# A two-layer network on attention output: the first sixteen feature steps issued from one written list of small pieces

## The chip, the core and the metric

The kernel runs on one core of a Trainium2 chip. The time is device time in microseconds (us) of one execution, taken as the median of the runs shown. A profile of one further execution gives the trace that is read here. Engines are named as in the profile: PE (matrix products), DVE (VectorE), ACT (ScalarE), POOL (GpSimd) and SP, whose queue issues nearly all DMAs.

## What is computed

Attention between 8 batches of 512 tokens and 32 state vectors per head, in both directions, then two feed-forward layers over all 8 x (512 + 32) = 4352 rows.

```
scores  = x @ state^T / 8;  a  = softmax(scores)      xread = a  @ state
scores2 = state @ x^T / 8;  a2 = softmax(scores2)     sread = a2 @ x
y = concat(xread, sread) as rows of 512
y = relu(y @ w_in)^2 @ w_out                          (512 -> 2048 -> 512, weights in float64)
h = y @ w2_in;  z = h * softmax(h)                    (512 -> 1024)
out = (z - mean) / sqrt(var + 1e-6) * g_ln @ w2_out   (1024 -> 512)
```

Every product keeps float32 accuracy by splitting each operand into a high and a low part and adding three products (high x high, high x low, low x high): lines 140, 141 and 142 of the kernel before.

## The kernel before, in words

**Layer 1, the feature steps.** The first layer is not applied to xread but to the attention weights: state @ w_in ("sw") is formed once per batch, so that the hidden values of a batch are a @ sw. There are 16 feature steps of 128 features for each batch. A step (b, f) has two parts. `hidden` makes six products of 128x512 into a bank `ps_h` (2 banks), ACT takes relu, then squares twice (`high`: `gh` and `r`), DVE subtracts (`low`: `gl`), and `project` multiplies `gh`, `gl` with four column blocks of w_out into four banks `acc` (twelve products). The steps of the first two batches alternate in chunks of four features: (0, 0 to 3), (1, 0 to 3), (1, 4 to 7), (0, 4 to 7) and so on. These first 16 steps are what the change is about. Each step's projection runs two steps behind its hidden product, so the work of the first 16 steps ends on PE with the fourteenth projection, just ahead of the seventeenth hidden product.

**Conversions.** w_in and w_out come as float64 words. A tile of 128x512 of them (0.5 MB) is converted by `convert_parts` in three parts: DVE does two masks and a multiply-add, ACT rebiases the exponent (`cz`); DVE joins the sign (`ch`), ACT writes the high part; DVE does a mask and a multiply for the low part. That is six DVE and two ACT instructions. 25 such conversions (13 of w_in, 12 of w_out) belong to the first 16 steps. Each converted w_in tile is also written to DRAM (`w1i_d`), and multiplied with the state (`sw_part`, products `ps_sw`, copied by ACT to `ev_sw` and stored to `sw_d`). `load_sw` reads a chunk of `sw_d` back into `stg`, and `split_sw` splits it (ACT high part, DVE low part) for the hidden products.

**Attention of a batch.** Transposes of x (`ps_x`), splitting (`xh`, `xl`, through a product with the negated identity, `negi`), scores (`ps_s`, copied to `st`), transposes by token (`ps_r`), row softmax (`rows_a`, `rows_b`, tiles `mx`, `e`, `sm`), transposes of the weights (`ps_a1`, shown as `ps_a`; split into `ah`, `al`), column softmax (`cols_a`, `cols_b`, tiles `cm`, `cs`), transposes of that (`ps_c`) and sread (`ps_sr`).

**Order.** The program is written as calls in a loop, and a scheduler of the framework decides the order on each engine, by its own estimates and by which buffers are free. Each engine then runs its instructions strictly in that order and waits where an operand is late. Layer 2 (line 743 on) comes after all 16 steps of 8 batches.

Of the kernel before, what the change touches and what calls it, by code (L numbers as in the profile page):

```python
# [8 lines left out]
F32 = mybir.dt.float32  # L9
# [11 lines left out]
def memory_attention_relu2_solu(  # L21
# [179 lines left out]
    def convert_parts(st, hi_r, lo_r, done=None):  # L201

        hi, lo = st[:, :, 1], st[:, :, 0]
        z = cvp.tile([P, 512], F32, tag="ce", name="cz")
        zu, zi = z.bitcast(U32), z.bitcast(I32)


        nc.vector.tensor_scalar(out=zu, in0=hi, scalar1=0x7FFFFE00, scalar2=None, op0=ALU.bitwise_and)
        nc.scalar.activation(out=zi, in_=zi, func=AF.Relu, scale=8.0, bias=rebias)

        u = cvp.tile([P, 512], F32, tag="cw", name="cu", bufs=4)
        uu = u.bitcast(U32)
# [90 lines left out]
    def sw_part(u, j):  # L303
# [106 lines left out]
        loading[b, c] = st  # L410

    def split_sw(b, c):
        st = loading.pop((b, c))
        loaded[b, c] = []
        for q in range(NQ):
            t = sw_tile("sw")
            split(t[:, 0, :], t[:, 1, :], st[:, q, :])
            loaded[b, c].append(t)

    def load_w1in(c, kk):  # L420
        for k in (2 * kk, 2 * kk + 1):
# [14 lines left out]
    def attention(b):  # L436

        v = {}

        def trans_x(hp):  # L440
            ps = bank("ps_x")
            transposes(ps, [xs_t[b][:, t, 2 * hp : 2 * hp + 2].rearrange("p h d -> p (h d)") for t in range(NT)])
            xh = xtp.tile([P, S], F32R, tag="xh", name="xh")
            xl = xtp.tile([P, S], F32R, tag="xl", name="xl")
            (split_bank if b < 2 else split)(xh, xl, ps)
            v["xt"] = (xh, xl)

        def scores_t(hp):
            xh, xl = v.pop("xt")
            q, i = hp // 2, hp % 2  # L450
            if i == 0:
                v["st", q] = atp.tile([P, S], F32, tag="st", name="st")
            if b < 2:
                if i == 0:
                    v["ps", q] = bank("ps_s")
# [90 lines left out]
                )  # L546

        def trans_a(q):
            if q == 0:
                a1_t[b] = (  # L550
                    a1p.tile([P, NQ, S], F32R, tag="ah", name="ah"),
                    a1p.tile([P, NQ, S], F32R, tag="al", name="al"),
                )
# [3 lines left out]
            (split_bank if b < 2 else split)(a1_t[b][0][:, q, :], a1_t[b][1][:, q, :], ps)  # L557

        def at(f, *a):
            return lambda: f(*a)  # L560
# [104 lines left out]
    fetch_pair(0, 0)  # L665
    load_x(0)
# [7 lines left out]
    fetch_pair(0, 1)  # L674
    fetch_pair(2, 0)
    fetch_pair(2, 1)
    fetch_w1out(0)
    att = attention(0)
    state_step(a_st, 0)
    load_x(1)  # L680
    for u in range(NM):
        begin("i", u)
        for k in range(5):
            advance()
            if k % 2 == 0 and len(att) > 5:
# [12 lines left out]
    begin("o", 0)
    load_state_rows(a_st, 2, B, nc.sync)
    state_step(a_st, 1)  # L700
    for u in range(NM):
        sw_part(u, 1)
        advance()
    while att:
        for piece in att.pop(0):
            piece()
    while flying:
        advance()
    nc.sync.dma_start(out=gcol, in_=g_ln.rearrange("(k p) -> p k", p=P))


# [103 lines left out]
    items += [(b, f) for b in range(2, B + 1) for f in range(NF)]  # L815
    chunks = [(b, c) for b, f in items if f % FPC == 0 for c in [f // FPC]]

    when = {("o", f): w for f, w in zip(range(1, NF), (0, 1, 2, 5, 6, 7, 8, 11, 12, 13, 14, 17, 19, 21, 22))}
    when |= {("i", u): w for u, w in zip(range(AHEAD, NU), (0, 1, 2, 3, 7, 8, 9, 10, 13, 15, 16, 18))}
    units = {}  # L820
    for unit, w in when.items():
        units.setdefault(w, []).append(unit)
# [10 lines left out]
            w2.append(t)  # L833

    done = []
    for s, (b, f) in enumerate(items):
        w, ws = divmod(s, NF)
        for kind, u in [unit for w_ in ((0, 1, 2) if s == 0 else (s + 2,)) for unit in units.get(w_, [])]:
# [37 lines left out]
        if s == 0:  # L876
            att = attention(1)
        if s in (11, 12):
            state_step(a_st, s - 9)
        if s == 2 * FPC - 2:  # L880
            load_sw(*chunks[2])
        for _ in range(4 if s < FPC else 1):
            if att:
                for piece in att.pop(0):
                    piece()
        if ws == 0 and 1 <= w < B - 1:
            load_x(w + 1)
        n = S if b < B else NSR
# [3 lines left out]
        done.append((b, f))  # L892
        if s // FPC + 1 < len(chunks) and chunks[s // FPC + 1][0] < B:
            nxt = chunks[s // FPC + 1]
            if s // FPC == 1:
                pass
            elif s % FPC == 1:
                if nxt not in loading:
                    load_sw(*nxt)
            elif s % FPC == 2:  # L900
                split_sw(*nxt)
        for e in ends.get(b, ())[1:]:
            i = f - e + 3
            if i not in (0, 1):
# [13 lines left out]
        for m in range(4):  # L918
# [5 lines left out]
                late_part(late, m - 2)  # L924
            if job:
                project(*job, m)
        if s == 2 * FPC - 1:
            split_sw(*chunks[2])
        if f == 0 and b == B - 1:
            sa.close()  # L930
            pools["x"] = pool("xp", 2, side="right")
# [69 lines left out]
```

## Time and profile before

| | |
|---|---|
| time, median of 3 runs (range) | 1135.21 us (1134.79 to 1138.87) |
| the profiled execution: its own time | 1133.88 us |
| its span in the trace | 1131.8 us |
| PE busy | 1102.5 us, 97% of the span |
| DVE busy | 704.0 us, 62% |
| ACT busy | 513.4 us, 45% |
| granted PE clock, mean of the span | 0.995 of full speed |

The span runs from the first to the last recorded event; the execution's own time has 2.1 us around it. Busy time of PE counts the modelled durations of its products, which overlap: a 128x512 product lasts 0.39 us, and the next one starts 0.23 us after it. So a busy PE may still be slow, when its clock is at the lower of its two levels (1.2 and 2.4 GHz; 0.5 and 1.0 in the profile).

### The profile page before, as it was taken

Reading aid. Unit: us, or ns where it says so; the run is one execution under the profiler, and the core shown is the slowest. Engines: PE = TensorE matmul, PEld = TensorE weight load, DVE = VectorE, ACT = ScalarE, POOL = GpSimd, SP = SyncE. Lnnn points to the kernel's source line nnn. Section 1 sums busy time; section 2 is a strip of 40 time slices with the busy share of each in tenths; the row PEclk is TensorE's granted clock in tenths of the full one; section 3 lists DMA queues with packets and bytes.
Section 4 is the critical chain, followed back from the end, with each engine's and each line's share of the span. In section 5 each row is a group of like instructions: output and inputs, shape, how many; then the busy total and the mean of one; then the engine's idle time right before and its main releaser. Section 6 shows DMA issues by size and latency. Waiting matters only on the chain.

```text
span 1131.8 us, 15153 instructions
## 1 busy us (share of the span) xinstructions
PE 1102.5 (97%) x5692; PEld 910.0 (80%) x5692; DVE 704.0 (62%) x1357; ACT 513.4 (45%) x903; POOL 44.7 (4%) x62
## 2 busy tenths in 40 slices
PE   5889999999999999999999999999999999999998
PEld 3667888888888888888888889988888888888886
DVE  6788886579477587784775446664545545445442
ACT  5878886456355353442343113443433434334332
POOL 1000000001000000010000000000000000000000
PEclk9899999999999999999999999999999999999999
DMA  9658874577666742422211127420101101000000
GB/s 291 236 177 280 298 238 135 168 225 216 208 208 174 210 146 75 140 75 60 72 38 57 38 75 256 153 75 19 61 24 57 66 19 45 21 19 28 19 28 28
DMA packets 92873, 134.69 MB, mean 119 GB/s; under 512 B 44800, under 2 KB 45312, under 8 KB 92800
## 3 DMA queue, kind: packets, MB, share of 16 engines
q1 hardware_dynamic: 92224, 133.59, 36.8%
q8 instruction: 45, 0.74, 0.3%
q14 instruction: 28, 0.23, 0.1%
q10 hardware_dynamic: 576, 0.13, 0.1%
HBM read 83.37 MB, written 49.28 MB: 117 GB/s over the span
## 4 chain that ended last, share of the span: by engine, by line
PE 91%; DVE 3%; ACT 3%; DMA 2%; issue 1%; SPq 0%; POOLq 0%; POOL 0%; ACTq 0%; DVEq 0%
PE h L750 16%; PE acc L140 11%; PE acc L141 10%; PE acc L142 10%; PE ps_h L140 6%; PE ps_h L141 6%; PE ps_h L142 6%; PE ps_o L801 5%; PE ps_o L799 5%; PE ps_o L800 5%; PE ps_t L789 2%; PE ps_sr L534 1%; PE ps_x L131 1%; DMA st<-in_moe_w_in_dram 1%; DMA st<-in_moe_w_out_dram 1%; PE ps_a L131 1%
## 5 line engine op out<-in xcount | busy, mean ns | idle before, releaser
L140 PE MATMUL acc<-gh,w1out 128*128 128x512 f32 (+1 forms) x576 | 218.8, 380 | 1.4 <-ACT ev_x L634 1.4
L141 PE MATMUL acc<-gl,w1out 128*128 128x512 f32 (+1 forms) x576 | 218.1, 379 | 0.0
L142 PE MATMUL acc<-gh,w1out 128*128 128x512 f32 (+1 forms) x576 | 217.8, 378 | 0.0
L750 PE MATMUL h<-w,x2h 128*128 128x512 f32 x544 | 148.6, 395 | 0.0
L593 ACT ACTIVATE r<-ps_h 128x512 f32<-128x512 f32 (+1 forms) x144 | 82.4, 573 | 141.2 <-PE ps_h L142 139.5
L595 DVE TENSOR_TENSOR r<-r,ps_h 128x512 f32<-128x512 f32 (+1 forms) x112 | 72.5, 647 | 88.9 <-ACT r L593 88.3
L140 PEld LDWEIGHTS acc<-gh,w1out 128*128 128x128 f32 x576 | 108.4, 188 | 22.3 <-ACT ev_x L634 1.8
L142 PEld LDWEIGHTS acc<-gh,w1out 128*128 128x128 f32 x576 | 108.4, 188 | 20.6
L141 PEld LDWEIGHTS acc<-gl,w1out 128*128 128x128 f32 x576 | 108.4, 188 | 20.0
L750 PEld LDWEIGHTS h<-w,x2h 128*128 128x128 f32 x544 | 99.6, 188 | 18.9
L609 DVE TENSOR_TENSOR gl<-r,gh 128x512 fp32r<-128x512 f32 (+1 forms) x144 | 96.5, 670 | 20.9 <-ACT r L602 17.9
L140 PE MATMUL ps_h<-ah,sw 128*128 128x512 f32 x256 | 107.8, 422 | 0.5 <-ACT r L593 0.5
L799 PE MATMUL ps_o<-w,lh 128*128 128x512 f32 x272 | 106.1, 390 | 1.0 <-ACT lh L119 1.0
L801 PE MATMUL ps_o<-w,ll 128*128 128x512 f32 x272 | 106.2, 390 | 0.6 <-DVE ll L120 0.6
L800 PE MATMUL ps_o<-w,lh 128*128 128x512 f32 x272 | 105.8, 389 | 0.0
L768 ACT ACTIVATE e<-h,nm 128x1024 f32<-128x1024 f32 x34 | 38.0, 1117 | 143.7 <-DVE nm L765 143.7
L141 PE MATMUL ps_h<-al,sw 128*128 128x512 f32 x256 | 101.3, 396 | 0.0
L142 PE MATMUL ps_h<-ah,sw 128*128 128x512 f32 x256 | 100.8, 395 | 0.0
L764 DVE TENSOR_REDUCE nm<-h 128x1 f32<-128x1024 f32 x34 | 41.6, 1225 | 84.4 <-PE h L750 84.4
L750 PE MATMUL h<-w,x2l 128*128 128x512 f32 x272 | 83.7, 389 | 0.0
L776 ACT ACTIVATE j<-e,mu 128x1024 f32<-128x1024 f32 x34 | 39.1, 1151 | 54.3 <-DVE mu L773 50.4
L801 PEld LDWEIGHTS ps_o<-w,ll 128*128 128x128 f32 x272 | 51.0, 188 | 12.0 <-DVE ll L120 1.5
(161 smaller groups left out, 1724.8 us busy)
## 6 DMA issues: line engine op xcount, KB each, us to landing
stg<-sw_d SPq DMA_DIRECT2D x120, 128.0 KB, 3.4
sw_d<-ev_sw SPq DMA_DIRECT2D x28, 512.0 KB, 3.7
st<-in_moe_w_out_dram SPq DMA_DIRECT2D x24, 512.0 KB, 5.2
xs<-in_x_dram SPq DMA_DIRECT2D x32, 256.0 KB, 4.0
w1i_d<-w1in SPq DMA_DIRECT2D x16, 512.0 KB, 4.5
st<-in_moe_w_in_dram SPq DMA_DIRECT2D x16, 512.0 KB, 5.8
w1in<-w1i_d SPq DMA_DIRECT2D x32, 256.0 KB, 4.7
x_d<-ev_x SPq DMA_DIRECT2D x16, 512.0 KB, 2.8
```

What stands on the lines that cost most here:

```text
L140: nc.tensor.matmul(out=ps, lhsT=lh, rhs=rh, start=first and i == 0, stop=False)
L141: nc.tensor.matmul(out=ps, lhsT=lh, rhs=rl, start=False, stop=False)
L142: nc.tensor.matmul(out=ps, lhsT=ll, rhs=rh, start=False, stop=last and i == n - 1)
L593: nc.scalar.activation(out=r, in_=ps, func=AF.Relu)
L595: nc.vector.tensor_tensor(out=r, in0=r, in1=ps, op=ALU.mult)
L609: nc.vector.tensor_tensor(out=gl, in0=r, in1=gh.bitcast(F32), op=ALU.subtract)
L750: nc.tensor.matmul(out=ps[:, a * 512 : (a + 1) * 512], lhsT=lt[:, k, t * P : (t + 1) * P], rhs=w2[k][:, i, a * 512 : (a + 1) * 512], start ...
L764: nc.vector.tensor_reduce(out=nm, in_=ps, axis=AX.X, op=ALU.max)
L776: nc.scalar.activation(out=j, in_=e, func=AF.Square, bias=mu, accum_out=var)
L799: nc.tensor.matmul(out=ps, lhsT=a, rhs=wt[:, 0, o : o + 512], start=(k == 0), stop=False)
L800: nc.tensor.matmul(out=ps, lhsT=a, rhs=wt[:, 1, o : o + 512], start=False, stop=False)
L801: nc.tensor.matmul(out=ps, lhsT=bb, rhs=wt[:, 0, o : o + 512], start=False, stop=(k == NK - 1))
```

## The change

Everything up to the end of the sixteenth feature step is no longer called in the loop, but from a written list of 304 entries. Each entry is one small piece, of a few instructions: a letter for the kind and hexadecimal digits for batch, step, unit or block. `T00` transposes the x of batch 0, pair of heads 0; `N00` is the second half of its split; `S` scores, `R` and `Q` the two halves of the row softmax, `A` and `B` the weights' transpose and the second half of its split, `C`, `D`, `E`, `F` the column direction; `i0` or `o0`, three times each, are the three parts of a conversion; `W10` is `sw_part` of unit 1 for j = 0; `V00` half a `split_sw`; `H`, `G`, `L` and `P` are `hidden`, `high`, `low` and one column block of `project`; `I`, `J`, `K`, `O`, `X`, `Z`, `l` are loads; `U` is a `state_step`. While the list is traced, PE, DVE, ACT and SP keep the list's order; later work is ordered by the scheduler as before, and may be put between entries of the list.

Banks and buffers change with it: the transposed x of the first two batches goes to the four `acc` banks (before: the two banks `m`), `sw_part` of the first four units to the `ps_h` banks (before: `acc` banks), `xh` and `xl` of batch 0 to buffers of `gh` and `gl`, those of batch 1 to that batch's `ah` and `al`, and `st` has four buffers (before: two). One conversion of w_in (unit 13) moves from the sixteenth step to the seventeenth. The load of `g_ln` now stands ahead of all other loads.

```diff
     def split_bank(hi, lo, ps):
 
         nc.scalar.activation(out=hi, in_=ps, func=AF.Copy)
-        nc.tensor.matmul(out=ps, lhsT=negi, rhs=hi, start=False, stop=True, skip_group_check=True)
-        nc.scalar.activation(out=lo, in_=ps, func=AF.Copy)
+
+        def rest():
+            nc.tensor.matmul(out=ps, lhsT=negi, rhs=hi, start=False, stop=True, skip_group_check=True)
+            nc.scalar.activation(out=lo, in_=ps, func=AF.Copy)
+
+        return rest
...
-        ps = ps_a.tile([P, 512], F32, tag=f"acc{hp}", name="ps_sw") if u < AHEAD and j < 2 else bank("ps_sw")
+        ps = ps_h.tile([P, 512], F32, tag="h", name="ps_sw") if u < AHEAD else bank("ps_sw")
...
         def trans_x(hp):
-            ps = bank("ps_x")
+            ps = ps_a.tile([P, 512], F32, tag=f"acc{hp}", name="ps_x") if b < 2 else bank("ps_x")
...
-    when = {("o", f): w for f, w in zip(range(1, NF), (0, 1, 2, 5, 6, 7, 8, 11, 12, 13, 14, 17, 19, 21, 22))}
-    when |= {("i", u): w for u, w in zip(range(AHEAD, NU), (0, 1, 2, 3, 7, 8, 9, 10, 13, 15, 16, 18))}
+    when = {("o", f): w for f, w in zip(range(12, NF), (20, 21, 22, 23))}
+    when |= {("i", u): w for u, w in zip(range(3 * AHEAD + 1, NU), (16, 17, 18))}
...
+    def piece(p):
+        k, a = p[0], [int(c, 16) for c in p[1:]]
+        if k in "TNSRQABCDEF":
+            att[a[0]][k](a[1])
...
+    PLAN = """
+    I0 X0 J0 I2 i0 J2 X1 i0 U0 O0 O1 T02 T00 i0 i1 N02 T03 i2 N00 Z W00 S02 T01 N03 i2 N01 i1 i1 S00 i3 S03
+    W10 i2 S01 T10 i3 i3 o0 W20 T11 N10 R00 o0 o1 W30 N11 I6 R01 o1 S10 T12 S11 Q00 Q01 I4 U1 o1 V00 V10 N12
+    A00 T13 o0 A01 B00 V00 V10 J4 B01 W01 N13 H00 O2 O3 i6 W11 G00 S12 H01 S13 i4 W21 i6 i6 L00 i5 W31 R10
...
+    with tc.manual_schedule(engines={getattr(mybir.EngineType, e) for e in ("PE", "DVE", "Activation", "SP")}):
+        for p in PLAN.split():
+            piece(p)
```

Three places show how the order on an engine moves. The first is PE ahead of the first hidden product (`ps_h`), before. `ps_a` is the transpose of the row softmax `e`, once for each half.

```order
L131 MATMUL ps_a_345<-ident,e_297 128x128 x2
L131 MATMUL ps_a_345<-ident,e_329 128x128 x2
L131 MATMUL ps_a_372<-ident,e_297 128x128 x2
L131 MATMUL ps_a_372<-ident,e_329 128x128 x2
L125 MATMUL ps_a_345<-ah,negi 128x512
L140 MATMUL ps_h<-ah,sw 128x512
L125 MATMUL ps_a_372<-ah,negi 128x512
L141 MATMUL ps_h<-al,sw 128x512
```

The same place of PE in the changed kernel, where lines have moved by 4 or more (L140 is L144, L131 is L135, L125 is L127).

```order
L135 MATMUL ps_a_464<-ident,e_380 128x128 x2
L135 MATMUL ps_a_464<-ident,e_410 128x128 x2
L135 MATMUL ps_x<-ident,xs 128x128 x4
L135 MATMUL ps_a_478<-ident,e_380 128x128 x2
L135 MATMUL ps_a_478<-ident,e_410 128x128 x2
L127 MATMUL ps_a_464<-ah,negi 128x512
L127 MATMUL ps_a_478<-ah,negi 128x512
L144 MATMUL ps_sw<-w1in,bd_1_155 128x512
L145 MATMUL ps_sw<-w1in,bd_1_155 128x512
L146 MATMUL ps_sw<-w1in,bd_1_155 128x512
L127 MATMUL ps_x<-ah,negi 128x512
L144 MATMUL ps_h<-ah,sw 128x512
```

The x of batch 1 (`ps_x`) and the first `sw_part` of the second state block (`bd_1`) now stand ahead of the first hidden product; before, all of batch 1's attention came after it. Ahead of these rows stand three more groups of batch 1's transposes, two of its score triples and the second `state_step`.

The second place is DVE at the same point, before: the end of the row softmax (`sm`, `e`), the low parts of the four `sw` tiles, the rest of a conversion, and three `low`.

```order
L498 TENSOR_SCALAR sm<-sm 128x16
L499 RECIPROCAL sm<-sm 128x16 x2
L500 TENSOR_TENSOR e_297<-e_297,sm 128x512
L500 TENSOR_TENSOR e_329<-e_329,sm 128x512
L516 RECIPROCAL cs<-cs 128x1
L120 TENSOR_TENSOR sw<-stg,sw 128x512 x4
L225 SCALAR_TENSOR_TENSOR w1out<-cu,cz 128x512
L609 TENSOR_TENSOR gl<-r,gh 128x512 x3
```

The same point of DVE in the changed kernel.

```order
L517 TENSOR_SCALAR sm<-sm 128x16
L518 RECIPROCAL sm<-sm 128x16
L519 TENSOR_TENSOR e_410<-e_410,sm 128x512
L120 TENSOR_TENSOR bd_1_155<-ps_st,bd_1_155 128x2x128
L120 TENSOR_TENSOR bd_1_158<-ps_st,bd_1_158 128x2x128
L228 TENSOR_SCALAR cz<-ch 128x512
L229 SCALAR_TENSOR_TENSOR w1out<-cu,cz 128x512
L120 TENSOR_TENSOR sw<-stg,sw 128x512 x2
L228 TENSOR_SCALAR cz<-ch 128x512
L229 SCALAR_TENSOR_TENSOR w1out<-cu,cz 128x512
L120 TENSOR_TENSOR sw<-stg,sw 128x512 x2
```

The column direction (`cs`, `cm`) has left this place for a later one, and the second `state_step` (`bd_1`) and two conversions of w_out finish ahead of the last `sw` split.

The third place is the start of SP's queue, before.

```order
L656 DMA st64w<-in_moe_w_in_dram 128x1024
L434 DMA xs<-in_x_dram 128x8x64 x4
L656 DMA st64w<-in_moe_w_in_dram 128x1024 x3
L163 DMA st_190<-in_moe_w_out_dram 128x1024
L434 DMA xs<-in_x_dram 128x8x64 x4
```

The start of SP's queue in the changed kernel.

```order
L697 DMA gcol<-in_moe_g_ln_dram 128x8x1
L681 DMA st64w<-in_moe_w_in_dram 128x1024
L441 DMA xs<-in_x_dram 128x8x64 x4
L681 DMA st64w<-in_moe_w_in_dram 128x1024 x3
L441 DMA xs<-in_x_dram 128x8x64 x4
L167 DMA st_217<-in_moe_w_out_dram 128x1024
L167 DMA st_219<-in_moe_w_out_dram 128x1024
```

`gcol` has come to the front, and the x of batch 1 has moved ahead of the first w_out tile.

## Rows read from the trace of the kernel before

**Rows 1.** The page: span, and busy time of each engine.

```profile
span 1131.8 us, 15153 instructions
PE 1102.5 (97%) x5692; PEld 910.0 (80%) x5692; DVE 704.0 (62%) x1357; ACT 513.4 (45%) x903; POOL 44.7 (4%) x62
```

**Rows 2.** Busy time by stretches; clock is a share of full, DMA of 16 engines.

```profile
core 0: us, PE busy (x) PEld busy (x) DVE busy (x) ACT busy (x) POOL busy (x), PEclk, DMA share, GB/s
0.00:7.21 7.21, 0.00 (x1) 0.04 (x1) 3.02 (x7) 2.72 (x4) 4.07 (x12) 1.00 0.84 203
7.21:26.13 18.92, 15.56 (x56) 9.76 (x56) 13.98 (x30) 12.75 (x26) 0.00 (x0) 1.00 1.06 334
26.13:30.90 4.77, 0.00 (x2) 0.03 (x1) 4.77 (x16) 3.81 (x8) 0.00 (x0) 0.83 0.98 308
68.86:72.18 3.32, 0.00 (x1) 0.03 (x1) 3.32 (x12) 1.62 (x3) 0.00 (x0) 1.00 0.00 0
138.57:200.00 61.43, 61.37 (x287) 50.43 (x286) 45.66 (x89) 44.47 (x80) 0.00 (x0) 1.00 0.60 189
200.00:1131.80 931.80, 925.75 (x4805) 772.17 (x4804) 546.79 (x1034) 361.14 (x623) 40.65 (x50) 1.00 0.30 94
```

**Rows 3.** The same view, from the first hidden product to the seventeenth.

```profile
33.44:138.57 105.13, 97.29 (x538) 75.65 (x537) 88.68 (x183) 86.81 (x163) 0.00 (x0) 0.97 0.71 238
```

**Rows 4.** The same view, PE alone, where its clock was low.

```profile
33.44:36.40 2.96, 2.96 (x9) 0.55 0.84 153
29.60:36.40 6.80, 5.50 (x17) 0.52 0.95 283
74.00:77.40 3.40, 3.26 (x9) 0.55 0.43 166
```

**Rows 5.** PE's waits, 0 to 260 us: for whom, total, times, longest.

```profile
PE ps_a L131 <- DVE e L500: 8.1, 2, 4.8
```

**Rows 6.** PE in order of time: start, duration, instruction.

```profile
33.44 0.63 PE L140 MATMUL ps_h<-ah,sw 128*128 128x512 f32 x1
...
112.85 0.60 PE L289 MATMUL ps_st<-ident,a_st 128*128 128x128 f32 x4
113.21 0.48 PE L140 MATMUL ps_h<-ah,sw 128*128 128x512 f32 x1
...
138.35 0.39 PE L142 MATMUL acc<-gh,w1out 128*128 128x512 f32 x1
138.57 0.39 PE L140 MATMUL ps_h<-ah,sw 128*128 128x512 f32 x1
```

**Rows 7.** DVE in order of time, with the idle time before and its cause.

```profile
10.98 0.43 DVE L208 TENSOR_SCALAR cz<-st64w 128x512 uint32<-128x512 uint32 x1 [1.73 <-DMA st64w<-in_moe_w_in_dram]
...
16.00 0.42 DVE L208 TENSOR_SCALAR cz<-st64w 128x512 uint32<-128x512 uint32 x1
16.34 0.42 DVE L224 TENSOR_SCALAR cz<-ch 128x512 uint32<-128x512 uint32 x1
...
18.68 0.69 DVE L507 TENSOR_REDUCE cm<-st 128x1 f32<-128x512 f32 x1 [0.98 <-ACT st L459]
19.28 0.68 DVE L214 SCALAR_TENSOR_TENSOR cu<-st64w,cu 128x512 f32<-128x512 uint32 x1
19.88 0.15 DVE L508 TENSOR_SCALAR cm<-cm 128x1 f32<-128x1 f32 x1
...
31.35 0.67 DVE L120 TENSOR_TENSOR sw<-stg,sw 128x512 fp32r<-128x512 f32 x1
35.69 1.90 DVE L120 TENSOR_TENSOR sw<-stg,sw 128x512 fp32r<-128x512 f32 x3 [3.67 <-ACT sw L119]
```

**Rows 8.** The same view, SP: the issue of the g_ln load.

```profile
30.62 0.57 SPq L709 DMA_DIRECT2D gcol<-in_moe_g_ln_dram  x1
```

**Rows 9.** DMA issues: count, KB each, median us from issue to landing.

```profile
stg<-sw_d SPq DMA_DIRECT2D x120, 128.0 KB, 3.4
sw_d<-ev_sw SPq DMA_DIRECT2D x28, 512.0 KB, 3.7
```

More of the change, by code (lines that the diff above doesn't have):

```diff
@@ L438, in attention, with new_a1 @@
         v = {}
+        def new_a1():
+            a1_t[b] = tuple(a1p.tile([P, NQ, S], F32R, tag=t, name=t) for t in ("ah", "al"))
         def trans_x(hp):
-            ps = bank("ps_x")
+            ps = ps_a.tile([P, 512], F32, tag=f"acc{hp}", name="ps_x") if b < 2 else bank("ps_x")
             transposes(ps, [xs_t[b][:, t, 2 * hp : 2 * hp + 2].rearrange("p h d -> p (h d)") for t in range(NT)])
[L443 to L446, printed above, removed]
+            if b == 0:
+                xh = gp.tile([P, S], F32R, tag="gh", name="xh")
+                xl = gp.tile([P, S], F32R, tag="gl", name="xl")
+            elif b == 1:
+                if hp == 0:
+                    new_a1()
+                xh, xl = (a1_t[b][k][:, hp % 2, :] for k in range(2))
+            else:
+                xh = xtp.tile([P, S], F32R, tag="xh", name="xh")
+                xl = xtp.tile([P, S], F32R, tag="xl", name="xl")
+            v["rest", "x", hp] = (split_bank if b < 2 else split)(xh, xl, ps)
+            v["xt", hp] = (xh, xl)
         def scores_t(hp):
-            xh, xl = v.pop("xt")
+            xh, xl = v.pop(("xt", hp))
             q, i = hp // 2, hp % 2
             if i == 0:
-                v["st", q] = atp.tile([P, S], F32, tag="st", name="st")
+                v["st", q] = atp.tile([P, S], F32, tag="st", name="st", bufs=4)
             if b < 2:
@@ L548, in trans_a @@
         def trans_a(q):
[L549 to L553, printed above, removed]
+            if q == 0 and b != 1:
+                new_a1()
             ps = bank("ps_a1")
@@ L835, in memory_attention_relu2_solu @@
     done = []
+    att = [attention(0), attention(1)]
+    steps = {}
+    hid, sq, ready, left = {}, {}, {}, {}
+    def piece(p):
+        k, a = p[0], [int(c, 16) for c in p[1:]]
+        if k in "TNSRQABCDEF":
+            att[a[0]][k](a[1])
+        elif k in "io":
+            key = k, a[0]
+            if key not in steps:
+                begin(*key)
+                steps[key] = flying.pop()
+            next(steps[key], None)
+        elif k == "U":
+            state_step(a_st, a[0])
+        elif k == "W":
+            sw_part(*a)
+        elif k == "V":
+            key = tuple(a)
+            if key not in steps:
+                steps[key] = split_sw(*key)
+            next(steps[key], None)
+        elif k == "H":
+            b, f = a
+            hid[b, f] = b, f, S, hidden(b, f, loaded[b, f // FPC], *a1_t[b], S)
+            done.append((b, f))
+        elif k == "G":
+            sq[a[0], a[1]] = high(*hid.pop((a[0], a[1])))
+        elif k == "L":
+            ready[a[0], a[1]] = low(*sq.pop((a[0], a[1])))
+        elif k == "P":
+            project(*ready[a[0], a[1]], a[2])
+            left[a[0], a[1]] = left.get((a[0], a[1]), NM) - 1
+        elif k == "Z":
+            load_state_rows(a_st, 2, B, nc.sync)
+        elif k == "O":
+            fetch_w1out(a[0])
+        elif k in "IJ":
+            fetch_pair(a[0], "IJ".index(k))
+        elif k == "K":
+            fetch_w1in(a[0])
+        elif k == "X":
+            load_x(a[0])
+        elif k == "l":
+            load_sw(*a)
+        else:
+            raise ValueError(p)
@@ new lines, in memory_attention_relu2_solu @@
+    P021 L10 G11 C00 i9 W71 H12 P030 ib L11 D01 H13 P031 i9 l11 D00 l01 P032 ib O4 P033 i9 U3 P100 P110 P101
+    ib G12 P111 L12 V11 V11 E00 P102 P103 P113 P112 V01 W90 P122 G13 i8 H14 E01 Ka L13 P120 G14 P121 C10 C11
+    o4 i8 P123 D10 O5 H15 L14 P131 o4 F00 i8 o4 V01 F01 G15 O6 O7 P130 W91 P133 D11 H17 P140 ia P132 o5 P142
+    G17 ia o5 o5 W80 P141 O8 W81 P143 L15 H16 P151 O9 ia o6 E11 L17 G16 E10 o6 P152 P153 Kc Wa0 o6 H04 o7 o8
+    P150 Wa1 Wb0 L16 o8 H05 o7 P160 o7 G05 P161 o8 Wb1 F10 Oa o9 P162 P163 L05 G04 o9 ic H06 L04 o9 Ob P170
@@ L875, in memory_attention_relu2_solu @@
             att = attention(w + 1)
-        if s == 0:
-            att = attention(1)
         if s in (11, 12):
             state_step(a_st, s - 9)
[L880 to L885, printed above, removed]
+        if att:
+            for part in att.pop(0):
+                part()
         if ws == 0 and 1 <= w < B - 1:
@@ L894, in memory_attention_relu2_solu @@
             nxt = chunks[s // FPC + 1]
[L895 to L897 removed]
+            if s % FPC == 1:
                 if nxt not in loading:
@@ L900, in memory_attention_relu2_solu @@
             elif s % FPC == 2:
-                split_sw(*nxt)
+                for _ in split_sw(*nxt):
+                    pass
         for e in ends.get(b, ())[1:]:
```

67 lines of the change are left out of this document (24 added, 43 removed).

## The prediction

> **What bounds the kernel now.** I first read the page: PE is busy for 97% of the span, DVE and ACT for far less [rows 1]. The kernel as a whole is bound by PE. PE's idle time is 1131.8 - 1102.5 = 29.3 us, and the next question is where it lies. The table by stretches answers it: from 200 us to the end PE is busy for 925.75 of 931.80 us, and from 138.57 to 200 for 61.37 of 61.43 [rows 2]. So some 23 us of the idle time lie ahead of 138.57 us, which is where the seventeenth hidden product starts [rows 6]: the work of the first sixteen steps, the very stretch that the list rewrites. 7.21 of it pass before PE has anything at all [rows 2], while the first loads and conversions run, and the change leaves that.
>
> The view of PE's waits names the largest of the rest: twice PE stands for the row softmax on DVE before it can transpose it, 8.1 us in all, 4.8 the longer [rows 5]. In the table these are the stretches 26.13 to 30.90, with no PE work, and 68.86 to 72.18 [rows 2]. After either of them the granted clock is near its lower level for a while (0.52 from 29.60 to 36.40, 0.55 from 74.00 to 77.40) [rows 4]. A reader should see two things there: a wait of PE costs its own length, and then again some of the work behind it.
>
> **The change, part by part.** PE's instructions for these steps stay the same; only one w_in conversion (no PE work of the first sixteen steps) moves behind. So the sum is about when PE can do the same work. I split at the first hidden product, at 33.44 us before [rows 6].
>
> *Behind it.* From there to the seventeenth hidden product the kernel before takes 105.13 us, with 97.29 busy [rows 3]: 7.84 us of waits. The low clock costs more inside: 2.96 us busy at 0.55 are worth 1.63 at full clock, so 1.33 are lost, and 3.26 at 0.55 lose 1.47 [rows 4]. Without waits and low clock it would be 105.13 - 7.84 - 2.80 = 94.5 us.
>
> *Moved ahead of it.* The list puts four groups of transposes of batch 1's x, one group of the state, two score triples, one sw triple and five products for splits ahead of the first hidden product: 20 transposes and 6 + 3 + 5 = 14 products of 512 columns. Four transposes take 113.21 - 112.85 = 0.36 us, a product 138.57 - 138.35 = 0.22 to 0.23 [rows 6]: 1.8 + 3.2 = 5.0 us. They run where PE had nothing to do, in the 4.77 us ahead of 30.90 and in what was left of the start [rows 2], so they are free there; without that cover they cost their 5.0. What stays behind is 94.5 - 5.0 = 89.5 us.
>
> *When the first hidden product can run.* It needs the low part of the last `sw` split on DVE. Before, DVE reaches its first such split at 31.35 [rows 7]. I take its waits up to there as they are, since the same loads and the same softmax gate it in both orders, and change only its work. Pitches, from one start to the next: 0.34 us for a mask, 0.60 for a two-operand instruction or a reduction [rows 7], so a conversion is 3 x 0.34 + 3 x 0.60 = 2.82. The list adds ahead of the last split: the last multiply of w_out tile 0 (0.60), all of w_out tile 1 (2.82), two halves of the state split (0.67, at 0.34 each) and the four splits (2.40), together 6.5. It takes out the column direction: two reductions and six instructions of one or two columns, 1.6 (1.2, and about 0.07 each; 0.15 each [rows 7] would make it 2.1). The wait of 3.67 us between the first split and the others [rows 7], for ACT, goes, since ACT's list has the four high parts ahead of the weights' splits or between them. `gcol`, now the first load, holds SP for 0.57 us [rows 8] and shifts the first loads by that. Sum: 31.35 + 6.5 - 1.6 + 0.6 = 36.85. Three products of that first hidden group can run before it, so I count the start as 36.85 + 0.1 - 3 x 0.23 = 36.2, 2.8 us later than before.
>
> *Sum without losses.* 36.2 + 89.5 = 125.7, against 138.57: 12.9 us gained.
>
> *Low clock, c.* PE still runs dry ahead of the first weights' transposes: what the list puts there is short (5.0 us) and DVE's row softmax ends only about 31 to 32. No row shows this idle time. From below: none, if it stays too short for the clock to fall. From above: a fall as long as the one from 29.60 to 36.40 [rows 4], wholly behind the transposes: 6.80 x 0.48 = 3.3 us. The idle time is nearest to the 4.77 us row, so I take what the fall cost behind the first hidden product before, 1.3. The second fall, at 74, goes with its wait, since batch 1's softmax now has the hidden products of batch 0 on PE beside it.
>
> *New waits behind the first hidden product, s.* Below: 0. Above: the 7.84 us of the order before [rows 3]. What speaks for more than nothing: PE, DVE and ACT now all follow one list. In those 94 us PE has 89.5 us of work; DVE 88.68 less 4.9 moved ahead, 83.8; ACT 86.81 [rows 3] less some 4, so 83. Three queues at 88% and more, in which each waiting instruction holds all behind it, lose something at handoffs. What speaks for less than before: both waits for the softmax (3.32 us of the 7.84 is one of them [rows 2]) now have other entries beside them. I take 3.
>
> *The rest.* The conversion moved behind costs DVE 2.82 us between 138.57 and 200, where DVE is busy for 45.66 of 61.43 us [rows 2]: nothing; without that slack 2.8. The four `st` buffers and the moved banks add no instruction. DMA moved 238 GB/s at 0.71 of its time between 33.44 and 138.57 [rows 3]; the same bytes in 93 us are 0.80, below the 0.98 and 1.06 of the start [rows 2], so I count nothing. Behind 200 us PE has its work in the same order, and shifts as a whole.
>
> Sum: 12.9 - 1.3 - 3 = 8.6 us. Against the profiled execution (1131.8 us span, 1133.88 its own time) that is 1125.3. The median of the runs is 1135.21, 1.3 higher, and I forecast for a median: **1126.6 us**.
>
> **The rivals.** *(1) The list covers all.* The idle time at the softmax stays short, the clock does not fall, and handoffs cost nothing: 12.9 us, 1122.3; if the DVE waits of 1.73 and 0.98 us in the start [rows 7] vanish as well, 15.6 us, 1119.6. For it: every wait in the rows has work that could fill it. Against it: DVE, not PE, sets the start, and its list is not shorter.
>
> *(2) The clock stays low from the start until behind the first hidden product.* The work on PE ahead of it would be 56 transposes, 10 split products and 11 triples: 5.0 + 2.3 + 7.6 = 14.9 us at full clock, 29.8 at half. From 7.21 that ends at 37.0, and the first six hidden products, at twice 0.23 each, end at 39.8 instead of some 37: 2.8 later, and another 3.4 us at half clock (as long as the one at 74 [rows 4]) lose 1.7. Gain 12.9 - 1.3 - 2.8 - 1.7 - 3 = 4.1: 1131.1. Against it: in the rows the clock was low behind stretches in which PE had nothing (26.13 to 30.90, 68.86 to 72.18 [rows 2, 4]). The Trainium skill, "TensorE: Matmul & The Clock Gate", Part 4: PE-mode transpose, says that transposes in PE's transpose mode do not count as busy time for the clock. By that rule the entries that fill the start with transposes would not hold the clock up, and this rival would come true. No row here separates transposes from idle time.
>
> *(3) The waits come back.* With three lists near 88%, s is 10 instead of 3: a gain of 1.6, 1133.6. For it: the order before already lost 7.84 in this stretch. Against it: those were few and long, not many.
>
> *(4) Slower: the round trip through DRAM.* In the list `V11`, the split of chunk (1, 1), stands on ACT and DVE, and all behind it there waits for the path from `W71` to `sw_d` (landing 3.7 us) and back to `stg` (3.4) [rows 9], with issues some 9 us. PE has 54 products and 8 transposes between `W71` and `H14`, the first that needs the chunk: 13 us. So it is covered by some 4 us. It would have to take 13 + 8.6 + 5.7 = 27 us to make the kernel measurably slower, three times what the rows show, by a backlog in SP's queue, whose order is fixed as well.
>
> That the change does nothing can be ruled out: the order on all engines differs from the first row.
>
> **How the numbers follow.** 0.5% is 5.7 us, about what a measurement of this kernel can tell from no change. Chances: forecast 0.52 (its own range 1122.5 to 1129.5), (1) 0.20, (2) 0.10, (3) 0.12, (4) 0.06. Faster is forecast and (1): 0.72; same is (2) and (3): 0.22; slower is (4): 0.06. The range goes from 1119.5, the better end of (1), to 1133.5, the end of (3); outside are (4), and a part of (3) and of (1).
>
> **What would show it.** The first `ps_h` product at 34 to 37 us with its group ending by 38; the seventeenth hidden product at 130 us (125.7 + 1.3 + 3); PE's waits between them at 3 us, none over 2; no low clock at the second softmax; DVE and ACT busy for 88% or more between the two. Wrong would be: a first hidden product behind 39 us, low clock beyond it, an ACT wait at `V11`, or the gain given back behind the list, as idle time of PE between it and 200 us.

## The result, and the profile after

The changed kernel takes 1121.12 us (median of 5 runs, 1119.70 to 1121.30); the kernel before, beside it, 1135.21 (1134.23 to 1138.87). The ratio is 0.9868 with a 95% interval of 0.985 to 0.9885: 14.1 us faster. The profiled execution took 1121.30 us, its span is 1119.5: 12.3 less than the span in [rows 1].

First the page: span and PE's busy time.

```profile
span 1119.5 us, 15144 instructions
PE 1099.0 (98%) x5692; PEld 911.1 (81%) x5692; DVE 708.5 (63%) x1357; ACT 512.0 (46%) x903; POOL 44.7 (4%) x62
```

PE's idle time is 1119.5 - 1099.0 = 20.5 us, where it was 29.3: 8.8 of the 12.3 us. The other 3.5 are busy time: the same 5692 instructions take less. The table of busy time by stretches, with the columns of [rows 2], shows where. The cuts are PE's first work (8.20), the first hidden product (38.96) and the seventeenth (125.75); the row from 30.20 is where the clock was low.

```profile
0.00:8.20 8.20, 0.00 (x0) 0.03 (x1) 2.54 (x5) 2.42 (x4) 4.06 (x12) 1.00 0.83 180
8.20:38.96 30.76, 24.48 (x99) 17.38 (x100) 26.47 (x53) 24.57 (x49) 0.00 (x0) 0.86 0.91 294
30.20:40.40 10.20, 8.35 (x23) 5.69 (x24) 9.25 (x20) 7.44 (x16) 0.00 (x0) 0.50 0.63 232
38.96:125.75 86.79, 86.75 (x504) 71.20 (x503) 82.44 (x169) 77.57 (x147) 0.00 (x0) 0.99 0.79 268
125.75:200.00 74.25, 74.20 (x359) 60.13 (x357) 58.35 (x113) 55.39 (x99) 1.01 (x1) 1.00 0.62 197
200.00:1119.50 919.50, 913.53 (x4740) 762.37 (x4736) 538.68 (x1022) 352.05 (x608) 39.58 (x50) 1.00 0.30 94
```

From the first hidden product to the seventeenth PE is busy for 86.75 of 86.79 us; in [rows 3] that stretch was 105.13 long, with 34 more instructions, which now stand ahead of it. The seventeenth comes 138.57 - 125.75 = 12.8 us earlier, about the whole gain of the span. The view of PE's waits, 0 to 260 us, now reads:

```profile
PE ps_st L293 <- DMA a_st<-in_state_dram: 8.2, 1, 8.2
PE ps_x L127 <- ACT ah L124: 1.8, 2, 1.0
PE ps_x L127 <- ACT xh L124: 1.1, 1, 1.1
PE ps_s L145 <- DMA stg<-ev_sw: 1.1, 1, 1.1
PE ps_a L135 <- DVE e L519: 1.1, 1, 1.1
PE ps_a L127 <- ACT ah L124: 0.5, 2, 0.4
PE ps_s L145 <- ACT xl L128: 0.4, 1, 0.4
```

The 8.1 us for the row softmax [rows 5] have become 1.1, and all seven lines lie ahead of the first hidden product. The second softmax has not become faster; it has company. On DVE in order of time, its first and its last instructions, before and then after:

```profile
66.61 1.29 DVE L485 TENSOR_REDUCE mx<-ps_r 128x16 f32<-128x512 f32 x2 [0.63 <-PE ps_r L475]
...
71.36 1.28 DVE L500 TENSOR_TENSOR e<-e,sm 128x512 f32<-128x512 f32 x2
```

```profile
46.51 0.69 DVE L504 TENSOR_REDUCE mx<-ps_r 128x16 f32<-128x512 f32 x1
...
54.45 0.69 DVE L519 TENSOR_TENSOR e<-e,sm 128x512 f32<-128x512 f32 x1
```

It takes 8.6 us (46.51 to 55.14), where it took 6.0 (66.61 to 72.64), and PE is busy all that time, with hidden products, `ps_sw` and `acc`. The table by stretches, PE alone, from the softmax's start to the transposes of its result:

```profile
46.51:55.61 9.10, 9.10 (x44) 1.00 0.70 262
```

The start is later than before. DVE and PE in order of time, at the first conversion, the second half of the first pair of loads, the last `sw` split, and the first hidden product:

```profile
5.86 0.43 DVE L212 TENSOR_SCALAR cz<-st64w 128x512 uint32<-128x512 uint32 x1 [4.47 <-DMA st64w<-in_moe_w_in_dram]
...
12.94 0.43 DVE L212 TENSOR_SCALAR cz<-st64w 128x512 uint32<-128x512 uint32 x1 [0.75 <-DMA st64w<-in_moe_w_in_dram]
...
37.67 1.29 DVE L120 TENSOR_TENSOR sw<-stg,sw 128x512 fp32r<-128x512 f32 x2 [0.26 <-ACT sw L119]
```

```profile
38.96 0.63 PE L144 MATMUL ps_h<-ah,sw 128*128 128x512 f32 x1
```

The load that DVE took up at 10.98 [rows 7] is taken up at 12.94, and the first hidden product starts at 38.96 instead of 33.44.

### The profile page after: what moved, and what is told of

Same layout as the page of the kernel before. It is cut to its first block, busy times and chain, and to the rows that moved or that the text cites. A ratio compares the mean times of both kernels' runs of the same rounds, so it can differ in the third digit from the quotient of the medians.

```text
span 1119.5 us, 15144 instructions
## 1 busy us (share of the span) xinstructions
PE 1099.0 (98%) x5692; PEld 911.1 (81%) x5692; DVE 708.5 (63%) x1357; ACT 512.0 (46%) x903; POOL 44.7 (4%) x62
## 4 chain that ended last, share of the span: by engine, by line
PE 92%; DVE 3%; DMA 2%; ACT 1%; issue 0%; SPq 0%; POOLq 0%; POOL 0%; ACTq 0%; DVEq 0%
PE h L738 16%; PE acc L144 11%; PE acc L145 11%; PE acc L146 11%; PE ps_h L144 6%; PE ps_h L145 6%; PE ps_h L146 6%; PE ps_o L789 5%; PE ps_o L787 5%; PE ps_o L788 5%; PE ps_t L777 3%; PE ps_sr L553 1%; DMA st<-x_d 1%; DMA st64w<-in_moe_w_in_dram 1%; PE ps_x L135 1%; PE ps_sw L388 1%
## 5 line engine op out<-in xcount | busy, mean ns | idle before, releaser
L144 PE MATMUL acc<-gh,w1out 128*128 128x512 f32 (+1 forms) x576 | 219.1, 380 | 0.0
L144 PEld LDWEIGHTS acc<-gh,w1out 128*128 128x128 f32 x576 | 108.4, 188 | 20.6 <-DVE gh L629 0.2
L144 PE MATMUL ps_h<-ah,sw 128*128 128x512 f32 x256 | 107.0, 418 | 0.0
```

The costliest lines, as they stand in the source:

```text
L144: nc.tensor.matmul(out=ps, lhsT=lh, rhs=rh, start=first and i == 0, stop=False)
```

## The experiments

Three theories can explain the gain. Theory A: holding the list's order fills PE's waits at the two softmaxes. Theory B: it is the banks. Theory C: it is the smaller pieces, in whatever order. All runs stand in one table; the last two columns are where the first and the seventeenth hidden product start in the profiled execution (us).

| run | median us (range) | ratio to before, 95% interval | first | 17th |
|---|---|---|---|---|
| before | 1135.21 (1134.23 to 1138.87) | | 33.44 | 138.57 |
| changed | 1121.12 (1119.70 to 1121.30) | 0.9868 (0.985 to 0.9885) | 38.96 | 125.75 |
| e3_banks_alone | 1129.66 (1128.31 to 1130.74) | 0.9942 (0.9927 to 0.9958) | 41.89 | 131.85 |
| e3a_x_banks | 1129.94 (1128.20 to 1130.71) | 0.9951 (0.9933 to 0.9968) | 33.82 | 136.35 |
| e2_free_order | 1125.70 (1124.93 to 1126.56) | 0.9908 (0.9893 to 0.9923) | 39.77 | 130.32 |
| e5_dve_act | 1118.56 (1118.00 to 1119.07) | 0.9856 (0.9841 to 0.987) | 36.27 | 124.90 |
| e6_batch1_behind | 1126.78 (1126.42 to 1127.64) | 0.9916 (0.99 to 0.9933) | 38.07 | 132.74 |
| e1_gcol_late | 1119.94 (1119.37 to 1121.12) | 0.9859 (0.9844 to 0.9873) | 37.84 | 124.61 |
| e7_fill_products | 1120.15 (1118.67 to 1122.75) | 0.9872 (0.9854 to 0.989) | 37.52 | 124.41 |
| e8_fill_transposes | 1119.85 (1119.22 to 1120.24) | 0.9867 (0.9852 to 0.9881) | 36.97 | 124.04 |
| e12_move_alone | 1120.74 (1120.00 to 1121.65) | 0.9871 (0.9856 to 0.9886) | 38.54 | 125.35 |
| c_after_again | 1122.30 (1122.18 to 1122.78) | 0.9885 (0.9871 to 0.99) | 39.03 | 125.45 |
| e11_free_fill | 1119.11 (1118.74 to 1119.57) | 0.9858 (0.9841 to 0.9875) | 35.92 | 124.49 |
| e10_best | 1120.70 (1120.54 to 1121.14) | 0.9871 (0.9856 to 0.9886) | 35.57 | 125.65 |

The changed kernel, measured twice, gave 1121.1 and 1122.3. A difference of about 1 us between runs of different groups is therefore not told apart. The positions in the last columns are then the better witness: in the two profiles of the changed kernel they agree within 0.3 us, while the rest behind the seventeenth hidden product took 993.8 us in one and 995.0 in the other.

**Banks, pieces, or order.** Four runs. The banks alone, in the kernel before:

```diff
-        ps = ps_a.tile([P, 512], F32, tag=f"acc{hp}", name="ps_sw") if u < AHEAD and j < 2 else bank("ps_sw")
+        ps = ps_h.tile([P, 512], F32, tag="h", name="ps_sw") if u < AHEAD else bank("ps_sw")
...
-            ps = bank("ps_x")
+            ps = ps_a.tile([P, 512], F32, tag=f"acc{hp}", name="ps_x") if b < 2 else bank("ps_x")
```

> The kernel before with the other banks alone: token transposes of the first two batches in accumulation banks, the first state products in a hidden-product bank; no pieces, no list. Theory A (order): 1133 to 1136.5 us, the PE wait for the row softmax of the second batch stays near 8 us. Theory B (banks): the token transposes no longer compete for the two small banks, 3 to 6 us come off, 1129 to 1132.

6.0 us came off, as theory B has it. The banks change the order too, since the scheduler goes by which buffers are free: 108 of PE's instructions now stand ahead of the first hidden product, where it was 65 before and is 99 in the changed kernel. The next run takes the second of the two edits alone:

> The kernel before with one of the two moves of banks: the token transposes of the first two batches in accumulation banks. (Both moves together took 1129.7 us against 1135.7.) If the token transposes' competition for the two small banks was what cost, all of the 6 us come here: 1129 to 1130.5. If it was the first state products in the accumulation banks, nothing comes: 1135 to 1136.5.

5.3 us: by the medians nearly all of it is the token transposes. The profiles are less clear: the seventeenth hidden product comes 6.7 us earlier with both moves and 2.2 with this one, so what the other move adds is not settled. What this one does can be read. PE in order of time, batch 1's four groups of transposes, before:

```profile
51.64 0.66 PE L131 MATMUL ps_x<-ident,xs 128*128 128x128 f32 x4
...
55.20 0.60 PE L131 MATMUL ps_x<-ident,xs 128*128 128x128 f32 x4
...
58.56 0.60 PE L131 MATMUL ps_x<-ident,xs 128*128 128x128 f32 x4
...
62.05 0.60 PE L131 MATMUL ps_x<-ident,xs 128*128 128x128 f32 x4
```

and with the token transposes in the `acc` banks:

```profile
48.70 0.71 PE L131 MATMUL ps_x<-ident,xs 128*128 128x128 f32 x5
...
50.15 0.55 PE L131 MATMUL ps_x<-ident,xs 128*128 128x128 f32 x3
...
52.94 0.60 PE L131 MATMUL ps_x<-ident,xs 128*128 128x128 f32 x4
...
54.13 0.60 PE L131 MATMUL ps_x<-ident,xs 128*128 128x128 f32 x4
```

With two banks for `ps_x`, `ps_s` and `ps_r`, a group stood 3.4 to 3.6 us behind the last; with four more the first two groups come together and the others 2.8 and 1.2 us behind. The softmax behind them begins on DVE at 64.39 instead of 66.61, and PE's second wait for a softmax is 1.59 instead of 3.33 us. That is 2.2 of the 2.9 us between the two profiled spans.

The third run keeps pieces, banks and list, but lets the scheduler place everything:

```diff
-    with tc.manual_schedule(engines={getattr(mybir.EngineType, e) for e in ("PE", "DVE", "Activation", "SP")}):
-        for p in PLAN.split():
-            piece(p)
+    for p in PLAN.split():
+        piece(p)
```

> The changed kernel with the same list, pieces and banks, but the list's order is not held on the engines: the scheduler places the instructions by its own estimates, as it did in the kernel before. Theory A (the gain is the held order, which puts other entries into the two softmaxes' gaps): the waits at the second softmax come back, PE waits 5 to 9 us in all between the first and the seventeenth hidden product, and the time is 1128 to 1135 us. Theory B (the gain is in the smaller pieces and the banks, whatever the order): PE waits under 2 us there, and the time is 1120 to 1123.

It fell between: 1125.7, so theories A and C each have a share. All that the change has beside the two moves of banks, with no order held, gives another 4.0 us (1129.7 to 1125.7). The pieces and the list as an order of writing are in that, and so are the other buffers, the moved conversion and `gcol`; only `gcol` is taken by itself, below. Holding the order gives another 3.4 to 4.6 (to 1122.3 or 1121.1). Theory A's waits did not come back where it said: between the first and the seventeenth hidden product PE is idle for 2.4 us, not 5 to 9, and when it needs the second softmax (`ps_a` at 61.67) it does not wait. The waits sit ahead of 47 us, as the view of PE's waits of this run shows:

```profile
PE ps_x L127 <- ACT ah L124: 4.6, 2, 3.1
PE ps_sw L144 <- ACT bd L119: 2.4, 1, 2.4
PE ps_h L144 <- ACT sw L119: 1.3, 1, 1.3
```

All are waits for ACT. So the fourth run holds the list on DVE and ACT alone:

```diff
-    with tc.manual_schedule(engines={getattr(mybir.EngineType, e) for e in ("PE", "DVE", "Activation", "SP")}):
+    with tc.manual_schedule(engines={getattr(mybir.EngineType, e) for e in ("DVE", "Activation")}):
```

> The changed kernel with the list's order held on DVE and ACT alone; PE and SP are placed by the scheduler. (Held nowhere it took 1125.7 us, held on all four 1121.1.) If the 4.6 us lie in the order of the splits and softmax on DVE and ACT, this takes 1121 to 1122.5; if PE's own order matters as much, 1123 to 1125; if PE's order was all, 1125 to 1126.5.

1118.6, below every band that was given. All of the held order's gain is there with DVE and ACT alone; neither was held by itself. Whether holding PE and SP as well costs anything is less sure. By the medians it is 2.5 or 3.7 us, by the ratios to before 1.4 or 3.3; of these only the second clears the intervals, and barely. The seventeenth hidden product comes 0.6 to 0.9 us earlier. In the table by stretches, PE alone, the changed kernel and then this run up to 36 us:

```profile
8.20:36.00 27.80, 21.70 (x94) 0.90 0.98 314
```

```profile
8.20:36.00 27.80, 23.22 (x97) 0.90 1.00 315
```

Placed by the scheduler, PE is busy for 1.5 us more there, and its first hidden product comes at 36.27, ahead of two pieces that the list puts before it (`B01` and `N13`, second halves of splits).

**Moved ahead is nearly free.** Ten entries of batch 1 go back behind the second hidden group (the rest of the list is the same, written in other lines):

```diff
-    W10 i2 S01 T10 i3 i3 o0 W20 T11 N10 R00 o0 o1 W30 N11 I6 R01 o1 S10 T12 S11 Q00 Q01 I4 U1 o1 V00 V10 N12
-    A00 T13 o0 A01 B00 V00 V10 J4 B01 W01 N13 H00 O2 O3 i6 W11 G00 S12 H01 S13 i4 W21 i6 i6 L00 i5 W31 R10
...
+    i2 N01 i1 i1 S00 i3 S03 W10 i2 S01 i3 i3 o0 W20 R00 o0 o1 W30 I6 R01 o1 Q00 Q01 I4
+    U1 o1 V00 V10 A00 o0 A01 B00 V00 V10 J4 B01 W01 H00 O2 O3 i6 W11 G00 H01 T10 T11 N10 N11
+    S10 T12 S11 N12 T13 N13 S12 S13 i4 W21 i6 i6 L00 i5 W31 R10 G01 i5 R11 P000 P001 J6 i5 L01
...
```

> The changed kernel with ten entries of the second batch (token transposes and their second halves of the split, scores; 5.0 us of PE at the full clock) moved back behind the second hidden group, where the kernel before had them. Theory: ahead of the first hidden product PE only waits for DVE and the loads, so that these pieces were free there: the first hidden product stays within 0.6 us of 38.96, the work behind it grows by 4 to 5 us, and the time is 1124.7 to 1126.3 us. Rival: the pieces hold the first hidden product back (their ACT work, some 4 us, stands ahead of that of the first batch): it comes at 36.5 to 37.5 and the time is 1122.3 to 1124.

The first hidden product came 0.9 us earlier, outside the 0.6 that the theory allowed and short of the rival's 1.5, and the kernel took 4.5 to 5.7 us more. So ahead of the first hidden product the pieces cost 0.9 us, and behind it they cost what the theory said and a little more. Without these pieces PE stands for the first softmax again:

```profile
31.40 0.66 PE L135 MATMUL ps_a<-ident,e 128*128 128x128 f32 x2 [4.21 <-DVE e L519]
```

**The load at the head of the queue.** The load of `gcol` becomes an entry `g` near the list's end:

```diff
-    nc.sync.dma_start(out=gcol, in_=g_ln.rearrange("(k p) -> p k", p=P))
...
+        elif k == "g":
+            nc.sync.dma_start(out=gcol, in_=g_ln.rearrange("(k p) -> p k", p=P))
...
-    P171 l02 P172 ic ic P173 U2 F11 P040 G06 oa P042 H07 ob Wc0 Wc1 P052 oa ob L06 oa P041 P050 ob P043 P051
+    P171 l02 P172 ic ic P173 U2 F11 P040 G06 oa P042 H07 ob Wc0 Wc1 P052 oa ob L06 oa P041 P050 ob g P043 P051
```

> The changed kernel with one edit: the load of gcol is an entry of the list near its end, so that it no longer stands ahead of the first weight and token loads on SP's queue. Theory: the load of gcol is what makes the first DVE conversion start at 5.86 instead of 4.58 us and that of the pair's second half at 12.94 instead of 10.98, and with them the first hidden product at 38.96. Then the first conversion is back at 4.6 (within 0.3), the first hidden product comes at 36.9 to 37.9, and the kernel takes 1119.0 to 1120.1 us, 1 to 2 less than the changed kernel's 1121.1. Rival: the loads come late for another reason (the order of the pairs and of x's loads on the same queue). Then the first conversion stays at 5.7 to 5.9, the first hidden product at 38.5 to 39.2, and the time at 1120.7 to 1121.5.

The first conversion on DVE, in this run:

```profile
4.89 0.43 DVE L212 TENSOR_SCALAR cz<-st64w 128x512 uint32<-128x512 uint32 x1 [3.50 <-DMA st64w<-in_moe_w_in_dram]
```

In the nine traces of list kernels with `gcol` in front it starts at 5.50 to 6.04, in the two that have it late at 4.74 and 4.89. So this load, 4 KB in pieces of 4 bytes, puts off the first weight load behind it by about 1 us. The first and the seventeenth hidden product come 1.1 us earlier, as the theory has it. The time, 1.2 us less, does not tell it from no change by itself.

**The clock.** PE's clock is low from 30.2 to 40.4 us in the changed kernel. Extra work, whose result is overwritten, fills the gaps ahead, once with products (shown) and once with transposes of a tile of x in the same place; `T13` moves ahead in both.

```diff
+            for _ in range({2: 4, 3: 10}.get(hp, 0) if b == 1 else 0):
+                nc.tensor.matmul(out=ps, lhsT=negi, rhs=w1u[0][:, 0, :], start=True, stop=True)
             transposes(ps, [xs_t[b][:, t, 2 * hp : 2 * hp + 2].rearrange("p h d -> p (h d)") for t in range(NT)])
...
-    W10 i2 S01 T10 i3 i3 o0 W20 T11 N10 R00 o0 o1 W30 N11 I6 R01 o1 S10 T12 S11 Q00 Q01 I4 U1 o1 V00 V10 N12
-    A00 T13 o0 A01 B00 V00 V10 J4 B01 W01 N13 H00 O2 O3 i6 W11 G00 S12 H01 S13 i4 W21 i6 i6 L00 i5 W31 R10
+    W10 i2 S01 T10 i3 i3 o0 W20 T11 N10 R00 o0 o1 W30 N11 I6 R01 o1 S10 T12 S11 Q00 Q01 I4 U1 T13 o1 V00 V10 N12
+    A00 o0 A01 B00 V00 V10 J4 B01 W01 N13 H00 O2 O3 i6 W11 G00 S12 H01 S13 i4 W21 i6 i6 L00 i5 W31 R10
```

> The changed kernel with extra PE work whose result is overwritten: ahead of two token transpose groups of the second batch 4 and 10 products of 512 columns (3.2 us at the full clock) in the same bank, and the last of these groups moved ahead of the conversions beside it, so that PE's idle time of 5.1 us between 24 and 37 us is partly filled. The low clock of the changed kernel lies at 30.2 to 40.4 us. Theory: it is PE's idle time that brings it, and filled time keeps it away or moves it; DVE's last sw split at 38.9 still sets the first hidden product, which comes at 38.0 to 39.0, and the gain is what is lost behind it, 0.5 to 1.3 us: 1119.8 to 1120.6. Rival: the clock falls as before and the extra products hold the chain back: the first hidden product at 40 to 42 and 1122 to 1124.

> The same fill with transposes instead of products: 10 and 25 of 128 columns, 3.2 us at the full clock as well. By the rule of the Trainium skill (TensorE: Matmul & The Clock Gate, Part 4: PE-mode transpose) they would not hold the clock up: the low clock would begin at 30.2 us or earlier, be as long as 10.2 us or longer, and the extra work at half clock would hold the chain back: 1121.5 to 1124 us. Rival: PE's clock goes by whether it is busy, whatever with: then the clock and the time are as in the run with products, within 0.5 us.

> The changed kernel with the last token transpose group of the second batch moved ahead as in the two runs with fill, and no fill. If the fill kept the clock up in those runs, the low stretch is back here at about 30 us and 6.8 to 10.2 us long, mean clock 0.995 to 0.996, 1120.5 to 1121.5 us. If the move alone did it, the mean clock is 0.998 or more as with the fill, and 1119.5 to 1120.3.

> The changed kernel as it is, for comparison on the same chip with the runs beside it: 1120.5 to 1121.5 us, low clock for 10.2 us.

The same stretch of PE in four runs (after the length: busy, count, clock, DMA share, GB/s): the changed kernel again, the move alone, products, transposes.

```profile
30.00:41.00 11.00, 8.36 (x27) 0.69 0.75 259
```

```profile
30.00:41.00 11.00, 7.69 (x23) 0.69 0.72 250
```

```profile
30.00:41.00 11.00, 8.54 (x34) 0.84 0.66 215
```

```profile
30.00:41.00 11.00, 8.82 (x48) 1.00 0.66 205
```

With the move alone the low stretch is there as in the changed kernel; with products half of it is left; with transposes it is gone. The mean granted clocks of the four executions of each run say the same less sharply: 0.997 in all four with the move alone, 0.998, 0.999, 0.997 and 1.000 with products, 1.000, 1.000, 0.998 and 0.998 with transposes. So PE's gaps bring the low clock here, and transposes hold it up as products do. The Trainium skill, "TensorE: Matmul & The Clock Gate", Part 4: PE-mode transpose, says that the full clock does not engage for transposes, since they do not count as busy in the same way; the measurement decides, and here it says otherwise. With the clock held (transposes) the first hidden product comes at 36.97, 2.0 us earlier than in the changed kernel and 1.6 earlier than with the move alone, the seventeenth 1.7 and 1.3. The times are 1.0 and 1.3 us lower than 1121.1, not told apart from it by the intervals. The move alone was 1.6 us faster than the changed kernel on the same chip, with the seventeenth product only 0.1 earlier. In the profiles the difference lies behind that product: 1.2 us, 0.8 of them waits of PE at 257 and 321 us for ACT's `ev_sw`, which the list does not order.

**Putting them together.** Transposes as fill with DVE and ACT alone held, and the same with SP held too and `gcol` late (shown is the held engines of the second):

```diff
-    with tc.manual_schedule(engines={getattr(mybir.EngineType, e) for e in ("PE", "DVE", "Activation", "SP")}):
+    with tc.manual_schedule(engines={getattr(mybir.EngineType, e) for e in ("DVE", "Activation", "SP")}):
```

> The list held on DVE and ACT alone (1118.6 us in an earlier run) with the fill of 10 and 25 transposes, which is extra work whose result is overwritten. If the gains add, 1117.2 to 1118.0 and no low clock from 16 us on; if the scheduler's PE order had already covered what the fill covers, 1118.3 to 1119.

> The list held on DVE, ACT and SP, PE placed by the scheduler, gcol's load late, and the same fill of transposes as extra work. If PE's freedom is what made holding DVE and ACT alone the faster, and gcol's load costs about 1 us of the start, 1116.0 to 1117.5. If SP's freedom was it, 1118.5 to 1120.

The gains do not add. The first is 3.2 us faster than the changed kernel on the same chip, with ranges far apart, but by its ratio (0.9858) it is what holding DVE and ACT alone gave (0.9856). The second fits neither of its bands: it is 1.6 us slower than the first, although its first hidden product comes 0.35 earlier; its seventeenth comes 1.2 later, with nine more of PE's instructions placed ahead of it. Its clock is low for 3.4 us once more, but that lies ahead of its first hidden product. In the profiles the loss lies behind the list: between 244 and 257 us PE waits 1.8 us for ACT's and DVE's steps of later batches, where the first run has 0.2 of such waits. Whether SP's held order brings them stays open.

## Why the prediction was right, and where it was not

The forecast was 1126.6, the measurement 1121.1: faster, as said, and inside the range, but 5.5 us below the forecast and below the forecast's own band (1122.5 to 1129.5). Span to span the sum was 8.6 and the gain 12.3. By its own steps:

- **The start, 36.2: wrong, 38.96.** DVE's last `sw` split ends at 38.96, where the sum had 36.85. DVE's busy time and its waits up to the splits, before and after (after the length: busy, count, clock, DMA share, GB/s):

```profile
0.00:31.35 31.35, 22.21 (x53) 0.97 1.00 301
```

```profile
0.00:38.96 38.96, 29.02 (x58) 0.89 0.90 270
```

Its busy time grew by 6.8 us, where the sum had 6.5 - 1.6 = 4.9: this term was mis-sized by 1.9. The instructions added are those that the sum names, but its pitches came from an order in which neighbours seldom need each other. In the list a small step often stands right behind the one it needs, and then it starts later, 0.72 us behind a reduction instead of 0.60:

```profile
23.91 0.68 DVE L504 TENSOR_REDUCE mx<-ps_r 128x16 f32<-128x512 f32 x1
24.63 0.69 DVE L507 TENSOR_TENSOR e<-ps_r,mx 128x512 f32<-128x512 f32 x1
```

DVE's waits grew by 0.8 (31.35 - 22.21 = 9.1 to 9.9), where `gcol` was counted at 0.6. The last 0.7 is PE's: three products were to run ahead of that split, but PE, at half clock, is busy with other pieces of the list until 38.96. So the low clock lies ahead of the first hidden product, where the sum took DVE alone as the gate. The runs that touch the start move it by 1.1 us (`gcol` late), 1.6 (clock held) and 0.9 (the ten entries moved back); these overlap and are not shares of one sum.
- **Moved ahead at no cost: right but for 0.9 us.** The run that moves the pieces back loses 4.5 to 5.7 us; their 5.0 were the estimate.
- **Work behind, 89.5: too long, the largest miss (3.4 us).** 86.79 less the 0.7 lost at half clock (38.96 to 40.40) is 86.1 for the same 504 instructions. This step took the busy time of before for work, and corrected it only where the granted clock was low. At full clock, too, busy time holds more than work next to a wait, as PE in order of time shows before:

```profile
37.32 0.62 PE L142 MATMUL ps_h<-ah,sw 128*128 128x512 f32 x2
38.40 0.50 PE L140 MATMUL ps_h<-ah,sw 128*128 128x512 f32 x1 [0.46 <-ACT r L593]
38.74 0.40 PE L141 MATMUL ps_h<-al,sw 128*128 128x512 f32 x1
```

The two products ahead of the wait count 0.62 us instead of 2 x 0.23, and the one behind it is followed after 0.34 instead of 0.23: 0.27 us beside the wait of 0.46. That such places, and changes between transposes and products, make up the whole 3.4 us is argued, not shown.
- **Low clock, 1.3 behind the first hidden product: 0.7.** One fall, none at the second softmax, as said. It lasts to 40.4, beyond the first hidden product, which the prediction counts among its signs of being wrong; what it cost there was still less than the sum had.
- **New waits, s = 3: 0.04.** DVE is busy for 82.44 and ACT for 77.57 of the 86.79 us (95% and 89%, as forecast), and yet PE is idle for 0.04 us: in this list three nearly full queues lose nothing at handoffs.
- **The sum.** Start 2.8 worse; behind it 89.5 + 1.3 + 3 = 93.8 forecast, 86.8 measured, 7.0 better; behind the seventeenth 0.5 worse: 8.6 - 2.8 + 7.0 - 0.5 = 12.3. The misses pull in opposite directions; that the total came out no further off is in part luck.
- **The banks at nothing: wrong as a cause.** They add no instruction, but alone give 5 to 6 us, by taking 2.2 us off the second softmax's start among others. Nor does the second softmax need a held order: placed freely, PE does not wait for it either. The sum held all the same, since it was made from PE's idle time, whatever filled it.
- **The rest: right.** DMA share 0.79 (0.80 forecast), and PE busy for 74.20 of 74.25 us where the moved conversion went.
- **The rivals.** The time is that of (1), the list covers all, and its handoffs cost nothing, but the clock did fall. (2) did not come: the clock is full from 13 to 30 us. (Ahead of that the granted clock reads 1.00 as well, but a product of 512 columns lasts 0.78 us at 12.50 and 0.40 at 13.36.) (3) is refuted by the wait view. For (4), ACT's wait on `stg` from `sw_d` is 0.3 us in all between the first and the seventeenth hidden product.

## What to carry to other kernels

A wait of the bounding engine for a chain of small steps elsewhere can be filled by other work, or shortened by the buffers that let the chain start sooner; here a two-line change of banks gave 5 to 6 of the 14 us. Try it before an order by hand. When the order is held, try holding it on the engines that feed the bound one alone: that was no slower here than holding it on all four (1118.6 us against 1121.1 and 1122.3). Busy time around waits and low clock is not all work; take the work from a stretch without either. Take an instruction's pitch from a place where its neighbours depend on each other as they will in the new order.

## What the runs showed of the hardware

With 35 transposes in PE's gaps the granted clock was 1.00 from 30 to 41 us in the profiled execution, where without them it was 0.69. The same kernel, profiled twice, had its clock low for 10.2 us (30.2 to 40.4) and for about 7 (32.9 to 39.7), with first hidden products 0.07 us apart. A 4 KB load in pieces of 4 bytes at the head of a queue put off the load behind it by about 1 us. On DVE an instruction that needs the 128x512 reduction right ahead of it started 0.72 us after that one; next to independent neighbours the spacing was 0.60.
